# Attention with squared ReLU and a gated unit in one kernel: loads of v issued tile by tile, tile 24 and two loads of z moved, and another order of work at the end

## The chip, the cores and the metric

The kernel runs on one core of one Trainium2 chip. The metric is device time of one execution in microseconds (us); lower is better. Inputs and outputs are float32.

## The reference

For 8 batches of 3200 rows, v and u have 256 columns and z has 64. The scores are z times z transposed, so they are symmetric; their squared ReLU is multiplied with v, and the result, multiplied by u, goes through a short causal convolution, a sigmoid gate and two 256x256 projections.

```python
scores = (1.0 / S) * np.matmul(z, z.transpose(0, 2, 1))
attn = np.maximum(scores, 0.0) ** 2
x = u * np.matmul(attn, v)
xp = zeros of 4 rows, then x
gate = sigmoid(sum over k of conv_w[k] * xp[:, k : k + S, :])     # 5 taps
out = (gate * (x @ w_val)) @ w_out
```

## The kernel before, in words

The 3200 rows of a batch are 25 tiles of 128 rows. Queries are handled in six main chunks of 4 tiles (512 columns), numbered 0 to 5, and a last tile, number 24, which is a chunk of its own (number 6, `ONE`). For each main chunk the keys are walked in pairs of tiles; such a pair is a step, so a chunk has 13 steps. The last main chunk of a batch (5) has 16, since the three steps of chunk 6, marked S, are mixed into it.

Every float32 operand is held as a high part (rounded to the fast float32 form, `fp32r`) and a low part (the remainder), and each product is three products of parts. ScalarE (ACT) makes the high parts by a cast, VectorE (DVE) the low parts by a subtraction. For the weights of attention these are the tiles `ah` and `al`, for v `v_hl`, for z `zhl`, for x `xh` and `xl`, for the gated value `gvh` and `gvl`.

Since the scores are symmetric, the kernel computes a block once, transposes it (`turned`), stores it to DRAM (`mir`) and fetches it back later as `m` for the chunk on the other side. `m_fetch` issues that fetch six steps before the block's use; ACT casts it and DVE makes its remainder three steps before the use.

The order of all work is written out by hand. `at_step(s, fn, ...)` puts small work behind step s, and every engine runs its instructions in program order. Nearly all DMAs are issued by one queue, SyncE's (SP). A load, cast or remainder is placed by these tables, as steps relative to the start of a chunk:

- `Z_FROM[b][c]`: the step, relative to the first step of batch b, at which chunk c of z is loaded (`z_load`, four issues through `blocks_load`, L161). Its transpose by DVE (`z_turn`, L215), its cast (`z_high`) and its remainder (`z_low`, L231) follow 3, 4 and 5 steps later, for batch 1 4, 5 and 6. All z loads of batches 1 to 7 use one buffer, `z_raw`.
- `V_LOAD`: the step, relative to the start of the last main chunk of the batch before, at which tiles of v are loaded (`v_load_at`, down to `v_rows`, L356), and whether into a small buffer `v_raw` or into one of 8 tiles that shares the buffers of `turned` (`v_raws`).
- `V_HIGH`: the same for the cast of pair i of v by ACT (`v_high`, L410); the remainder by DVE (`v_low`, L415) follows one step later. Entry 12 is tile 24. For batch 1, steps above 13 count one more.

`v_rows` loads m neighbouring tiles of v with rows interleaved in blocks of 32: one issue for each of the four blocks of partitions.

The two chunks before are finished beside the attention of the current one: product with u, convolution taps (`conv`, L811), sigmoid, value product, gate, projection. The single tiles are finished in groups of batches (`one_...`). After the last steps of the last batch, the end is written out step by step: the last four steps' products are made for the left and the right 256 columns apart, so that the taps of the left half run beside the products of the right half; then value, gate, projection of the last chunk, the projection of the chunk before (`project_whole`, L972) and that of the last single tile.

Of the kernel before, what the change touches and what calls it, by code (L numbers as in the profile page):

```python
# [11 lines left out]
ALU = mybir.AluOpType  # L12
P = 128
BLK = 32
# [3 lines left out]
def attn_glu_kernel(  # L18
# [29 lines left out]
    nc = tc.nc  # L48
    B, S, D = u.shape
# [11 lines left out]
    sizes = [4] * n_chunks + [1]  # L61
    firsts = [4 * c for c in range(n_chunks + 1)]
# [13 lines left out]
    def f32(ap):  # L76
        return ap.bitcast(F32)
# [273 lines left out]

    def v_rows(dst, b, g, t, m):

        for a in range(P // BLK):
            k = firsts[g] * P + (a * sizes[g] + t) * BLK
            nc.sync.dma_start(  # L356
                dst[a * BLK : (a + 1) * BLK], v[b, k : k + m * BLK, :].rearrange("(t r) d -> r t d", r=BLK)
            )
# [78 lines left out]
    turned = {}  # L437
# [298 lines left out]
    u_raw, ut = {}, {}  # L736
# [21 lines left out]
    def gated(b, c, h, cols=ALL, with_=None):  # L758
        opened = (b, c) in xs
        if not opened:  # L760
            xs[b, c] = sb.tile([P, DH, X_ROW], F32, name="x", bufs=1)
        x = xs[b, c]
        nc.vector.tensor_tensor(  # L763
            x[:, h, HALO + cols.start : HALO + cols.stop], accs[b, c][h][:, cols] if with_ is None else with_, ut[b, c][:, h, cols], op=ALU.mult
        )
        if not opened:
            x_halo(b, c)
# [20 lines left out]
    def x_high(b, c, hs=slice(0, DH), cols=ALL):  # L788
        if (b, c) not in xhl:
            xhl[b, c] = (  # L790
                sb.tile([P, DH, CW], F32R, name="xh", bufs=1),
                sb.tile([P, DH, CW], F32R, name="xl", bufs=1),
            )
        nc.scalar.copy(xhl[b, c][0][:, hs, cols], xs[b, c][:, hs, HALO + cols.start : HALO + cols.stop])
# [7 lines left out]
    def conv(b, c, h, k, first=None, cols=ALL):  # L802
        x, cw = xs[b, c], weights["conv"]
        if (b, c) not in gates:
            gates[b, c] = sb.tile([P, DH, CW], F32, name="gate", bufs=1)
        g = gates[b, c][:, h, cols]
        tap = x[:, h, k + cols.start : k + cols.stop]
        if k == 0:
            (first or nc.scalar.mul)(g, tap, cw[:, h, 0:1])  # L809
        else:  # L810
            nc.vector.scalar_tensor_tensor(g, tap, cw[:, h, k : k + 1], g, op0=ALU.mult, op1=ALU.add)  # L811
# [44 lines left out]
    def value_part(b, c, h, cols, banks):  # L856
        wh, wl = weights["val"]
        xh, xl = (x[:, h, cols] for x in xhl[b, c])
        for terms in (((wl, xh), (wh, xh)), ((wh, xl),)):
            for e in range(DH):  # L860
                for wp, xp in terms:
                    ends = h == DH - 1 and xp is xl
                    nc.tensor.matmul(
                        banks[e][:, : CW // 2], wp[:, h, e * P : (e + 1) * P], xp, start=h == 0 and wp is wl, stop=ends
                    )
# [9 lines left out]
        nc.scalar.copy(gvs[b, c][0][:, e, cols], gv)  # L875
        return gv

    def gate_part_low(b, c, e, cols, gv):
        gvh, gvl = (x[:, e, cols] for x in gvs[b, c])
        nc.vector.tensor_tensor(gvl, gv, f32(gvh), op=ALU.subtract)  # L880

    def project_tiles(b, c, tiles_, banks):
        wh, wl = weights["out"]
# [79 lines left out]
    def project_whole(b, c, banks):  # L963
        pos[b, c] = banks
        lists = [project_list(b, c, x, True, True) for x in range(DH)]

        n = sizes[c]
        early = [3 if turned_out(b, c) else 3 * (n // 2 + (x == 0) * (n % 2)) for x in range(DH)]
        for part in range(2):
            for mms, e in zip(lists, early):  # L970
                for out_, st, mv, first, last in mms[e:] if part else mms[:e]:
                    nc.tensor.matmul(out_, st, mv, start=first, stop=last)  # L972
# [335 lines left out]
    def fill_at(s, fn, *args):  # L1308
# [23 lines left out]
    }  # L1332
    FIRST_LAST = {6: 9, 7: 10, 8: 11, 9: 12, 10: 12}

    Z_FROM = {b: (-53, -48, -41, -33, -22, -10, -15) if b > 1 else (-17, -40, -35, -31, -24, -9, -5) for b in range(1, B)}

    U_LOAD = ((6, -1, -8, -11, -8, -8), (1, -2, -2, -9, -8, -8))
    U_PREP = ((11, 2, 1, 2, 4, 6), (10, 10, 3, 4, 4, 6))
# [2 lines left out]
        (-9, (20, 21, 22, 23), None),  # L1341
        (-6, (14, 15, 16, 17), None),
        (2, (0, 1, 2, 3), (0, 0)),
        (3, (24,), (1, 6)),
        (4, (4, 5, 6, 7), (0, 4)),
        (6, (8, 9, 10, 11), (1, 0)),
        (8, (12, 13), (1, 4)),
        (16, (18, 19), None),
    )
    V_HIGH = (7, 8, 9, 10, 11, 12, 13, 16, 17, 18, 14, 15, 6)  # L1350

    CONVERSIONS = (
        (2, 2, convert_conv(), 10),
# [117 lines left out]
    with tc.manual_schedule():  # L1471
# [13 lines left out]
        for s in range(min(todo), END + 1):  # L1485
# [86 lines left out]
            if s == END:  # L1572

                b, c = LAST
                g = len(GROUPS) - 1
                assert (b, c) not in xhl and (b, c) not in gates
                one_products(g, (0, 1, 2))
                left_, right = slice(0, CW // 2), slice(CW // 2, CW)
                pending, sums = [], []
                for cols in (left_, right):  # L1580
                    for h in range(DH):
                        attend_part(steps[s:], h, cols, None if cols is left_ else apart[h][:, : CW // 2])
                        if cols is left_ and h == 0:
                            one_value_whole(g)
                            apart = two_banks(False)
                        if cols is left_:
                            gated(b, c, h, cols)
                        else:
                            nc.vector.tensor_tensor(sums[h], apart[h][:, : CW // 2], sums[h], op=ALU.add)
                            gated(b, c, h, cols, sums[h])  # L1590
                        x_high(b, c, one[h], cols)
                        if cols is left_ and h == 0:
                            one_value_copy(g)
                            one_products(g, (3, 4))
                        for fn, *args in pending:
                            fn(*args)
                        if cols is right:
                            one_halo_last(b, h)
                        conv(b, c, h, 0, nc.scalar.mul if (cols is left_) == (h == 1) else nc.vector.tensor_scalar_mul, cols)
                        if (cols, h) == (right, 1):  # L1600
                            break
                        if cols is left_:
                            sums.append(sb.tile([P, CW // 2], F32, name="sum", tag=("z_raw", "u_raw")[h], bufs=1))
                            nc.scalar.copy(sums[h], accs[b, c][h][:, right])
                        for k in range(1, KW):
                            conv(b, c, h, k, cols=cols)
                        sigmoid(b, c, one[h], cols)
                        pending = [(x_low, b, c, one[h], cols)]
                value_l, value_r = (s_bank_pair(x) for x in (next_s[0], 1 - next_s[0]))
                for h in range(DH):  # L1610
                    value_part(b, c, h, left_, value_l)
                value_part(b, c, 0, right, value_r)
                conv(b, c, 1, 1, cols=right)
                x_low(b, c, one[1], right)
                value_part(b, c, 1, right, value_r)
                project_whole(b, c - 1, two_banks(False))
                lefts = [gate_part(b, c, e, left_, value_l, "a") for e in range(DH)]
                one_conv_first(g)
                for k in range(2, KW):
                    conv(b, c, 1, k, cols=right)  # L1620
                sigmoid(b, c, one[1], right)
                one_sigmoid(g)
                for e in range(DH):
                    gate_part_low(b, c, e, left_, lefts[e])
                rights = [gate_part(b, c, e, right, value_r, ("gv", "zz")[e]) for e in range(DH)]
                one_gated_last(g)
                one_gated_high(g)
                for e in range(DH):
                    gate_part_low(b, c, e, right, rights[e])
                one_gated_low(g)  # L1630
                for x in range(DH):
                    out_copy(b, c - 1, x)
                out_store(b, c - 1)
                lefts = s_bank_pair(next_s[0])
                project_tiles(b, c, (0, 1), lefts)
                tiles_out(b, c, (0, 1), lefts, ("z_raw", "u_raw"), (nc.scalar.copy,) * 2, (nc.sync,) * 2)
                rights = two_banks(True, "acc")
                project_tiles(b, c, (2, 3), rights)
                one_project_whole(g, s_bank_pair(1 - next_s[0]))
                tiles_out(b, c, (2, 3), rights, ("ut", "turned"), (nc.vector.tensor_copy, nc.scalar.copy), (nc.scalar, nc.scalar))  # L1640
                one_out(g)


# [31 lines left out]
```

## Time and profile before

| what | value |
|---|---|
| median of 3 runs | 2258.09 us (2257.62 to 2263.52) |
| the profiled execution | 2262.12 us, span 2260.3 us |
| granted TensorE clock | 1.000 |
| DVE, ACT, POOL busy | 82%, 76%, 3% of the span |
| SP's waits of at most | 15.0 us (L542, for a `turned` tile) |
| loads of v of 64 KB and 32 KB | 100 + 28 and 28 + 4 issues |

In rows of the timeline the first number is the start in us from the start of the span, the second the duration; then come engine, line, operation, tile written and tiles read, and their shapes; `x4` means four instructions merged. In brackets stands how long the engine was idle before and what released it. SPq is SP's queue, PEld a weight load of TensorE. In rows of waits stand the engine and line that waited, whom for, and us in total, how often, and the longest. In rows of DMA issues the median time from issue to landing stands last.

### The profile page before, as it was taken

How to read it: one execution, taken by the hardware profiler on the slowest of the kernel's cores; microseconds unless marked ns; L12 is line 12 of the kernel's file. 1: busy time of each engine (PE TensorE's matmuls, PEld its weight loads, DVE VectorE, ACT ScalarE, POOL GpSimd, SP SyncE). 2: the span in 40 equal slices, each digit the busy share in tenths (PEclk: the TensorE clock that was granted, in tenths of full speed). 3: DMA queues.
4: the chain of work that ended last, by engine and by line, in shares of the span. 5: the costliest groups of instructions: out<-in, count | busy, mean ns of one | idle time of the engine just before them, and what ended most of it. 6: DMA issues, size and time to landing. Idle time of an engine off the chain costs nothing.

```text
span 2260.3 us, 50037 instructions
## 1 busy us (share of the span) xinstructions
PE 2247.4 (99%) x20311; PEld 1911.3 (85%) x20311; DVE 1852.5 (82%) x2296; ACT 1707.4 (76%) x2145; POOL 76.6 (3%) x119
## 2 busy tenths in 40 slices
PE   9999999999999999999999999999999999999998
PEld 7888888889888988888988888888898888888888
DVE  8877788887889778887888968888788887888776
ACT  8987688766887668876688766987669776697764
POOL 0000000000000000000000000000000000000000
PEclk9999999999999999999999999999999999999999
DMA  5557857887677876788667776777858778677663
GB/s 123 117 135 159 205 136 164 184 197 205 150 163 181 189 200 150 169 185 193 182 164 168 189 185 177 166 177 183 206 144 184 173 181 206 148 184 172 170 179 98
DMA packets 700600, 386.61 MB, mean 171 GB/s; under 512 B 411856, under 2 KB 635088, under 8 KB 700368
## 3 DMA queue, kind: packets, MB, share of 16 engines
q1 hardware_dynamic: 699024, 383.01, 71.4%
q8 instruction: 159, 2.61, 0.5%
q14 instruction: 73, 0.60, 0.1%
q10 hardware_dynamic: 1344, 0.39, 0.1%
HBM read 211.82 MB, written 171.44 MB: 170 GB/s over the span
## 4 chain that ended last, share of the span: by engine, by line
PE 92%; SPq 2%; DVE 2%; DMA 2%; ACT 1%; issue 1%; ACTq 0%; DVEq 0%
PE acc L428 67%; PE s L428 12%; PE misc L428 11%; DMA m<-mir 1%; SPq L356 1%; DVE al L649 1%; PE acc L733 1%; SPq L161 1%; SPq L1044 0%; DVE gate L811 0%; DMA z_raw<-in_z_dram 0%; DMA v_raws<-in_v_dram 0%; ACT ah L643 0%; SPq L555 0%; DVE x L763 0%
## 5 line engine op out<-in xcount | busy, mean ns | idle before, releaser
L428 PE MATMUL acc<-ah,v_hl 64*128 64x512 f32 x9472 | 1606.9, 388 | 1.2 <-DVE x L763 0.6
L428 PEld LDWEIGHTS acc<-ah,v_hl 64*128 64x128 f32 x9472 | 942.9, 184 | 165.0 <-issue 1.5
L428 PE MATMUL acc<-al,v_hl 64*128 64x512 f32 x4736 | 965.0, 387 | 2.1 <-DVE al L649 2.0
L428 PEld LDWEIGHTS acc<-al,v_hl 64*128 64x128 f32 x4736 | 480.9, 184 | 83.6 <-DVE al L649 4.8
L649 DVE TENSOR_TENSOR al<-a,ah 128x1024 fp32r<-128x1024 f32 (+1 forms) x346 | 398.3, 1151 | 184.5 <-ACT ah L643 182.7
L640 ACT ACTIVATE a<-s 128x1024 f32<-128x1024 f32 (+1 forms) x346 | 333.0, 963 | 137.5 <-PE s L428 122.8
L643 ACT CAST ah<-m 128x1024 fp32r<-128x1024 f32 x254 | 264.9, 1047 | 154.4 <-PE acc L428 83.0
L641 ACT ACTIVATE a<-a 128x1024 f32<-128x1024 f32 (+1 forms) x346 | 347.7, 1005 | 11.0
L649 DVE TENSOR_TENSOR al<-m,ah 128x1024 fp32r<-128x1024 f32 x254 | 307.8, 1212 | 53.7 <-ACT ah L643 53.6
L643 ACT CAST ah<-a 128x1024 fp32r<-128x1024 f32 (+1 forms) x323 | 319.9, 990 | 10.2
L520 DVE STREAM_TRANSPOSE turned<-a 128x1024 f32<-128x1024 f32 (+1 forms) x278 | 318.5, 1146 | 0.1
L811 DVE SCALAR_TENSOR_TENSOR gate<-x,cw,gate 128x512 f32<-128x512 f32 (+1 forms) x392 | 284.7, 726 | 4.9 <-ACT gate L809 1.1
L428 PE MATMUL s<-zq,zhl 64*128 64x512 f32 (+1 forms) x1596 | 222.5, 378 | 1.6 <-DVE gv L1065 1.6
L428 PEld LDWEIGHTS s<-zq,zhl 64*128 64x128 f32 x1596 | 153.0, 184 | 30.0 <-DVE gv L1065 2.0
L763 DVE TENSOR_TENSOR x<-acc,ut 128x512 f32<-128x512 f32 (+1 forms) x96 | 61.4, 681 | 83.4 <-PE acc L428 70.5
L815 ACT ACTIVATE gate<-gate 128x512 f32<-128x512 f32 (+1 forms) x98 | 60.9, 622 | 71.1 <-DVE gate L811 70.8
L913 ACT CAST gvh<-gv 128x512 fp32r<-128x512 f32 x94 | 58.2, 620 | 38.0 <-DVE gv L909 37.9
L428 PE MATMUL misc<-xh,w_val_hi 64*128 64x512 f32 x376 | 77.2, 386 | 0.0
L428 PE MATMUL misc<-xh,w_val_lo 64*128 64x512 f32 x376 | 77.2, 386 | 0.0
L428 PE MATMUL misc<-xl,w_val_hi 64*128 64x512 f32 x376 | 77.2, 386 | 0.0
L428 PE MATMUL s<-v_hl,ah 64*128 64x512 f32 x400 | 76.3, 394 | 0.0
L909 DVE TENSOR_TENSOR gv<-misc,gate 128x512 f32<-128x512 f32 x94 | 64.5, 686 | 12.7 <-PE misc L428 8.3
(197 smaller groups left out, 2021.7 us busy)
## 6 DMA issues: line engine op xcount, KB each, us to landing
mir<-turned SPq DMA_DIRECT2D x460, 256.0 KB, 4.1
m<-mir SPq DMA_DIRECT2D x230, 512.0 KB, 4.9
u_raw<-in_u_dram SPq DMA_DIRECT2D x384, 64.0 KB, 3.5
mir<-turned SPq DMA_DIRECT2D x376, 64.0 KB, 2.5
m<-mir SPq DMA_DIRECT2D x94, 256.0 KB, 4.6
out_dram<-ob SPq DMA_DIRECT2D x152, 128.0 KB, 3.6
v_raws<-in_v_dram SPq DMA_DIRECT2D x100, 128.0 KB, 3.7
z_raw<-in_z_dram SPq DMA_DIRECT2D x182, 64.0 KB, 3.2
```

The lines of the kernel that those rows point to most:

```text
L161: queues[i % len(queues)].dma_start(dst[i * BLK : (i + 1) * BLK], src[:, d0 : d0 + BLK].rearrange("(j c) r -> c j r", c=BLK),)
L428: ins = nc.tensor.matmul(out_, st[r], mv[r], start=first, stop=last)
L520: nc.vector.transpose(into[:, t : t + m], a[:, j * w : (j + m) * w].rearrange("p (t m x) -> p t m x", t=m, x=BLK))
L640: nc.scalar.activation(a[:, : n * w].rearrange("p (j x) -> p j x", j=2), s[:, :, :each], AF.Relu, scale=scale)
L641: nc.scalar.activation(a, a, AF.Square)
L643: nc.scalar.copy(hi, a)
L649: nc.vector.tensor_tensor(lo, a, f32(hi), op=ALU.subtract)
L763: nc.vector.tensor_tensor(x[:, h, HALO + cols.start : HALO + cols.stop], accs[b, c][h][:, cols] if with_ is None else with_, ut[b, c][:, h ...
L811: nc.vector.scalar_tensor_tensor(g, tap, cw[:, h, k : k + 1], g, op0=ALU.mult, op1=ALU.add)
L815: nc.scalar.activation(g, g, AF.Sigmoid)
L909: nc.vector.tensor_tensor(gv[:, :w], pvs[b, c][e][:, :w], gates[b, c][:, e, :w], op=ALU.mult)
L913: nc.scalar.copy(gvs[b, c][0][:, e, :w], gv_[b, c, e][:, :w])
```

## The change

It does four things.

1. `v_rows` has a new path for runs shorter than 4 tiles: one issue for each tile, with all 128 partitions, in place of one for each block of 32 partitions.
2. Tile 24 of v is loaded with tiles 18 and 19 at step 16, the first step of the next batch, into `v_raw`, and no longer at step 3 of the last chunk; its cast goes from step 6 to step 19.
3. For batch 1, the load of z for chunk 0 goes from step -17 to step -15, and that for chunk 6 from step -5 to step -20. Their transposes, casts and remainders follow.
4. At the end: the tap 0 that ACT makes goes ahead of the cast of xh; the projection of the chunk before (`project_whole`) goes between the value products of the left and the right half; the remainders of the left gated value go from DVE to GpSimd (POOL); the third tile's projection is stored before the single tile's projection, on SP, and the fourth's comes last, copied by DVE.

```diff
     def v_rows(dst, b, g, t, m):
+        if m < P // BLK:
+            for x in range(m):
+                k = firsts[g] * P
+                rows_ = v[b, k : k + sizes[g] * P, :].rearrange("(a t r) d -> t a r d", t=sizes[g], r=BLK)[t + x]
+                nc.sync.dma_start(dst[:, x], rows_)
+            return
         for a in range(P // BLK):
...
-    def gate_part_low(b, c, e, cols, gv):
+    def gate_part_low(b, c, e, cols, gv, engine=nc.vector):
         gvh, gvl = (x[:, e, cols] for x in gvs[b, c])
-        nc.vector.tensor_tensor(gvl, gv, f32(gvh), op=ALU.subtract)
+        engine.tensor_tensor(gvl, gv, f32(gvh), op=ALU.subtract)
...
-    Z_FROM = {... else (-17, -40, -35, -31, -24, -9, -5) ...}
+    Z_FROM = {... else (-15, -40, -35, -31, -24, -9, -20) ...}
...
-        (3, (24,), (1, 6)),
...
-        (16, (18, 19), None),
+        (16, (18, 19, 24), None),
     )
-    V_HIGH = (7, 8, 9, 10, 11, 12, 13, 16, 17, 18, 14, 15, 6)
+    V_HIGH = (7, 8, 9, 10, 11, 12, 13, 16, 17, 18, 14, 15, 19)
...
+                        on_scalar = (cols is left_) == (h == 1)
+                        if on_scalar:
+                            conv(b, c, h, 0, nc.scalar.mul, cols)
                         x_high(b, c, one[h], cols)
...
-                        conv(b, c, h, 0, nc.scalar.mul if (cols is left_) == (h == 1) else nc.vector.tensor_scalar_mul, cols)
+                        if not on_scalar:
+                            conv(b, c, h, 0, nc.vector.tensor_scalar_mul, cols)
...
                     value_part(b, c, h, left_, value_l)
+                project_whole(b, c - 1, two_banks(False))
                 value_part(b, c, 0, right, value_r)
                 conv(b, c, 1, 1, cols=right)
                 x_low(b, c, one[1], right)
                 value_part(b, c, 1, right, value_r)
-                project_whole(b, c - 1, two_banks(False))
...
-                    gate_part_low(b, c, e, left_, lefts[e])
+                    gate_part_low(b, c, e, left_, lefts[e], nc.gpsimd)
...
-                project_tiles(b, c, (2, 3), rights)
+                project_tiles(b, c, (2,), rights[:1])
+                tiles_out(b, c, (2,), rights[:1], ("ut",), (nc.vector.tensor_copy,), (nc.sync,))
                 one_project_whole(g, s_bank_pair(1 - next_s[0]))
-                tiles_out(b, c, (2, 3), rights, ("ut", "turned"), (nc.vector.tensor_copy, nc.scalar.copy), (nc.scalar, nc.scalar))
+                project_tiles(b, c, (3,), rights[1:])
                 one_out(g)
+                tiles_out(b, c, (3,), rights[1:], ("turned",), (nc.vector.tensor_copy,), (nc.scalar,))
```

More of the change, by code (lines that the diff above doesn't have):

```diff
@@ L1333, in attn_glu_kernel @@
     FIRST_LAST = {6: 9, 7: 10, 8: 11, 9: 12, 10: 12}
-    Z_FROM = {b: (-53, -48, -41, -33, -22, -10, -15) if b > 1 else (-17, -40, -35, -31, -24, -9, -5) for b in range(1, B)}
+    Z_FROM = {b: (-53, -48, -41, -33, -22, -10, -15) if b > 1 else (-15, -40, -35, -31, -24, -9, -20) for b in range(1, B)}
     U_LOAD = ((6, -1, -8, -11, -8, -8), (1, -2, -2, -9, -8, -8))
```

## The prediction

> **What bounds the kernel now.** I read the page first, then the waits of PE, then the timeline of PE at the few places where it waits, and from each place back along ACT, DVE and SP. The page says that TensorE is the bound almost everywhere:
>
> ```profile
> span 2260.3 us, 50037 instructions
> PE 2247.4 (99%) x20311; PEld 1911.3 (85%) x20311; DVE 1852.5 (82%) x2296; ACT 1707.4 (76%) x2145; POOL 76.6 (3%) x119
> ```
>
> No product is added or removed by the change, so only PE's idle time, and the work behind the last product, can be won. The waits of PE (who was waited for: us in total, times, longest) set the ceiling:
>
> ```profile
> PE acc L428 <- DVE al L649: 2.0, 3, 0.8
> PE s L428 <- DVE gv L1065: 1.6, 1, 1.6
> PE misc L435 <- DVE zeros L1473: 1.5, 1, 1.5
> PE s L863 <- DVE xl L798: 0.6, 1, 0.6
> PE acc L428 <- DVE x L763: 0.6, 3, 0.2
> ...
> ```
>
> That is 6.3 us in the rows shown, 1.5 of it the first memset, which stays. 0.3% of 2258 is 6.8 us, about what a measurement of this kernel can tell from no change; even a perfect edit hardly reaches it. PE's timeline shows where the idle time lies (start, duration, form, idle before and its releaser):
>
> ```profile
> 270.05 0.39 PE L428 MATMUL s<-v_hl,al 64*128 64x256 f32 x2 [0.29 <-DVE al L649]
> 272.78 0.50 PE L428 MATMUL acc<-al,v_hl 64*128 64x512 f32 x2 [0.82 <-DVE al L649]
> 278.54 0.38 PE L428 MATMUL s<-v_hl,al 64*128 64x256 f32 x2 [0.18 <-DVE al L649]
> 289.58 0.73 PE L428 MATMUL s<-zq,zhl 64*128 64x512 f32 x4 [1.58 <-DVE gv L1065]
> 1396.22 0.50 PE L428 MATMUL acc<-al,v_hl 64*128 64x512 f32 x2 [0.38 <-DVE al L649]
> 1673.29 0.50 PE L428 MATMUL acc<-al,v_hl 64*128 64x512 f32 x2 [0.76 <-DVE al L649]
> ```
>
> Four of the six, 2.87 us, lie in the last chunk of batch 0, where batch 1 is fetched; the other two, 1.14 us, at the same place before batches 5 and 6. All six come late in the last chunk, and the ACT and SP rows of that place say why:
>
> ```profile
> 246.09 1.05 ACT L643 CAST ah<-m 128x1024 fp32r<-128x1024 f32 x1 [4.09 <-DMA m<-mir]
> 267.31 0.41 ACT L410 CAST v_hl<-v_raws 128x256 fp32r<-128x256 f32 x1 [7.08 <-DMA v_raws<-in_v_dram]
> 233.87 4.85 SPq L356 DMA_DIRECT2D v_raw<-in_v_dram  x8
> 246.49 3.33 SPq L161 DMA_DIRECT2D z_raw<-in_z_dram  x4
> 262.12 2.90 SPq L356 DMA_DIRECT2D v_raws<-in_v_dram  x4
> 278.77 3.36 SPq L356 DMA_DIRECT2D v_raws<-in_v_dram  x4
> 282.86 2.08 SPq L161 DMA_DIRECT2D z_raw<-in_z_dram  x4
> ```
>
> The 0.41 us cast of tile 24 (128x256) held ACT's queue for 7.08 us, because its four loads were issued only at 262.12 on a late SP queue. Behind it in ACT's order stood the casts whose al PE missed at 270.05 and 272.78.
>
> **The change part by part.**
>
> *Loads of v by tile.* One issue per tile of 128 rows replaces four per run of one or two tiles: in batches 1 to 7, 20 issues become 9 (runs 14-15, 16-17, 12-13, 18-19, and 24); in batch 0, 20 become 9 as well. Before tile 14, 8 issues took 4.85 us; 4 at the same 0.61 take 2.4, and SP is 2.4 us earlier for the mirror fetches behind. 12-13 saves half of 3.36, 1.7 us.
>
> What such a load costs until it lands, no row shows: a source of four blocks of 32 rows in one issue does not occur. The nearest are the 32-row and 64-row loads:
>
> ```profile
> v_raws<-in_v_dram SPq DMA_DIRECT2D x28, 32.0 KB, 3.3
> q1 hardware_dynamic: 699024, 383.01, 71.4%
> ```
>
> Lower end: it lands like these, 3.3 us after issue, and the saved issues are a gain. Upper end: its four blocks are served four wide. From the queue row (packets, MB, share of 16 engines), 0.714 x 16 x 2260.3 us for 383 MB is 67 ns of one DMA engine for each KB; a 131 KB tile is 8.8 engine-us, 0.55 us over 16 engines and 2.2 us over four. I take the lower end for my sum, with something kept for the start, since most landing times are waits and not transfer; the upper end is rival one. The Trainium skill, "DMA: Bandwidth & Descriptors", section "Why a DMA increments its semaphore by 16 and not by 1", has a rule that speaks for the upper end: a transfer uses the largest number of engines up to 16 that divides the outermost dimension of both sides. By it a source of four blocks would run on four engines; nothing in this trace shows such a transfer, so it stays a rival.
>
> *At the start* the loads feed DVE:
>
> ```profile
> 3.05 2.03 SPq L356 DMA_DIRECT2D v_raw<-in_v_dram  x4
> 6.65 0.43 DVE L410 CAST v_hl<-v_raw 128x512 fp32r<-128x512 f32 x1
> 8.92 0.69 DVE L231 TENSOR_TENSOR zhl<-misc,zhl 128x512 fp32r<-128x512 f32 x1 [1.11 <-ACT zhl L226]
> 18.52 0.42 DVE L410 CAST v_hl<-v_raw 128x512 fp32r<-128x512 f32 x1
> ```
>
> Tiles 0 and 1 are cast at 6.65, and DVE then idles 1.11 us, which covers that much lateness. Two issues instead of four end 1.0 us earlier. Gain to -0.3; loss at four engines: eight tiles, 17.6 us in a row from 3.05, end at 20.7 at the earliest, and at 24 with the 3.3 us to land; the last pair is cast at 18.52, so 2 to 5 late. I take +0.3.
>
> *Tile 24.* Its load leaves SP at step 3 of the last chunk (2.90 us there) and joins 18 and 19 at step 16; cast and remainder move from steps 6 and 7 to 19 and 20. ACT's 7.08 us wait goes; late next are the mirror casts behind it, which wait for their own fetches, and those are issued earlier by the 2.9 us. The price is 0.41 us on ACT and 0.42 on DVE in the next first chunk, and one more tile behind 18-19. There the cover is:
>
> ```profile
> 578.92 0.79 SPq L356 DMA_DIRECT2D v_raw<-in_v_dram  x2
> 585.17 0.63 ACT L410 CAST v_hl<-v_raw 128x512 fp32r<-128x512 f32 x1
> ```
>
> 6.25 us from the first issue to the cast, against 3.3 to land and 0.6 for each issue: hidden, and tile 24 has one step more. If that cover went, the 0.8 us of casts would cost up to 0.4 a batch.
>
> *Two z loads of batch 1.* Chunk 0's load (four issues, 3.33 us) goes from before the last chunk to step 1 of it, chunk 6's (2.08 us) from step 11 of the last chunk to step 9 of the chunk before. SP's order then: chunk 6's four issues stand before the first mirror fetch of the last chunk, whose cast at 246.09 began as its DMA landed, so a delay there passes on. It is 2.08 late against 2.4 early from tiles 14 to 17: nothing. Everything behind 246.49 moves 3.3 us forward up to step 1, where the load now stands. Its transpose on DVE moves two steps:
>
> ```profile
> 254.46 0.71 DVE L215 STREAM_TRANSPOSE zz<-z_raw 128x512 f32<-128x512 f32 x1
> 261.04 0.69 DVE L231 TENSOR_TENSOR zhl<-zz,zhl 128x512 fp32r<-128x512 f32 x1
> ```
>
> The transpose will stand about where the remainder stood, 261.0. It took at most 8.0 us from first issue (246.49) to transpose; from an issue at 250 to 254 it is ready at 258 to 262: DVE waits 0 to 1 us, and the remainders of the mirrors wait behind it. The z work of chunk 6, operands a quarter of chunk 0's, moves into the last chunk.
>
> Joint: between -2.9 (all four idle times go) and +1.0 (none goes and the transpose waits). The 1.58 at 289.58 hangs on the last mirror fetches, behind 278.77 and 282.86; SP is lighter there by 2.9 + 1.7 us ahead of them, so I take -2.9 in the profiled run. Before batches 5 and 6 the same ACT wait goes: -1.1, or 0.
>
> *The end.*
>
> ```profile
> 2240.51 2.05 DVE L811 SCALAR_TENSOR_TENSOR gate<-x,cw,gate 128x256 f32<-128x256 f32 x4 [0.55 <-ACT gate L809]
> 2244.23 2.05 DVE L811 SCALAR_TENSOR_TENSOR gate<-x,cw,gate 128x256 f32<-128x256 f32 x4 [0.55 <-ACT gate L809]
> 2247.46 0.51 PE L863 MATMUL s<-xl,w_val_hi 128*128 128x256 f32 x2 [0.63 <-DVE xl L798]
> 2237.44 0.72 POOL L1161 TENSOR_TENSOR one_sum<-one_sum,one_terms 128x248 f32<-128x248 f32 x1 [1.91 <-ACT one_terms L1159]
> 2237.55 0.89 DVE L811 SCALAR_TENSOR_TENSOR gate<-x,cw,gate 128x256 f32<-128x256 f32 x1
> 2256.69 0.66 SPq L1267 DMA_DIRECT2D out_dram<-one_f  x1
> ```
>
> Twice DVE waits 0.55 us for ACT's gate product, because ACT casts xh first. With the order turned DVE starts up to 0.55 earlier each time, I take 0.4, 0.8 in all; xh has PE's remaining sums ahead of it. Putting the 24 products of the chunk before between the halves of the value hides the 0.63 of 2247.46. Moving two remainders to POOL takes 0.75 off DVE and puts two operations of about 0.72 on POOL; but beside a POOL operation a tap took 0.89, where four take 2.05 (0.51 each), so up to 0.4 for each of two comes back. The third tile's output now precedes the single tile's, which overlaps copies. The last store, 2256.69, moves forward by the 0.63 and part of the 0.8. Bounds -1.3 and +0.3; I take -0.8. The Trainium skill, "SBUF — State Buffer", section "SBUF: two separate sides", says that such a VectorE operation with two inputs in SBUF and a GpSimd operation exclude each other, the second one waiting in full. By it 0.7 would come back for each and the end would gain 0.3; the trace agrees with a wait, and its 0.4 decides.
>
> **Sum.** The profiled execution took 2262.12 us (span 2260.3). -2.9 - 1.1 - 0.8 + 0.3 = -4.5: 2257.6 on that footing. The median of the runs is 2258.09, 4.0 lower, as much as the six idle times together, and two of these stand at only two of seven like places; so I credit the median with half of them: 2258.1 - 2.0 - 0.8 + 0.3 = **2255.6**.
>
> **The rivals.**
>
> One, slower: the one-issue tiles are served by four engines. Place: the start, and each last chunk's first mirror fetch, which follows tiles 14 to 17.
>
> ```profile
> 1064.40 3.78 SPq L356 DMA_DIRECT2D v_raw<-in_v_dram  x8
> 1073.28 1.05 ACT L643 CAST ah<-m 128x1024 fp32r<-128x1024 f32 x1 [1.57 <-DMA m<-mir]
> 1077.15 1.22 DVE L649 TENSOR_TENSOR al<-m,ah 128x1024 fp32r<-128x1024 f32 x1
> 1079.60 0.61 PE L428 MATMUL acc<-al,v_hl 64*128 64x512 f32 x2
> ```
>
> Four tiles hold four engines for 8.8 us instead of 2.2; less 1.9 of saved issuing, the fetch lands up to 4.7 us later. ACT's cast starts as it lands and ends at 1074.33, DVE uses it at 1077.15: 2.8 are covered. It decides from there; up to 1.9 us pass on to the remainder, which ends at 1078.37 and is used by PE at 1079.60, 1.2 later: 0 to 0.7 a batch, I say 0.5 in six. With +2.5 at the start and my other terms: 2258.1 + 3 + 2.5 - 2.8 = 2260.8.
>
> Two, nothing happens in the middle: runs without a profiler have few of these waits, and the gain is the end's: 2258.1 - 0.8 + 0.3 = 2257.6. For it speaks that only batch 1 waits for more than a microsecond; against it, ACT's 7.08 us is a queue order and not chance.
>
> Three, all of it is won in the median too: 2258.1 - 4.0 - 1.3 - 0.3 = 2252.5.
>
> **How the numbers follow.** Forecast 0.50, four engines 0.25, nothing in the middle 0.13, all won 0.12. All four lie within 0.3% (2251.3 to 2264.9). Slower than that takes the upper ends of rival one (5 at the start, 0.7 in six batches and no gain elsewhere: 2267.3): 0.07. Faster takes more than PE's removable idle time: 0.05. Same: 0.88. The range reaches from a little below "all won" to the middle of rival one: 2251.8 to 2261.
>
> **What would show it.** Right: no ACT wait for v_raws near 260 to 267, PE without idle at 269 to 290, DVE's waits for the gate product gone from the end, SP issuing 72 small loads of v and not 160. Wrong: landing times of the 128 KB v loads far above the 64 KB ones, new PE idle within the first 25 us or near the first mirror fetches, a DVE transpose of z waiting for its DMA near 261, or taps near 0.9 us beside POOL until PE waits in the last products.

## The result, and the profile after

| kernel | median | ratio to before (95% interval) |
|---|---|---|
| before | 2258.09 us (2257.62 to 2263.52) | |
| after | 2282.9 us (2280.9 to 2285.64) | 1.0103 (1.009 to 1.0117) |

The change makes the kernel 24.8 us slower; the prediction was 2255.6 us, 2261 at the most. In what follows, each ratio, and each "over" or "under before" of a median, is against runs of the kernel before made beside the kernel named (medians 2258.09 to 2260.13 us); one run of both_old_loads, 2787.72 us at a granted clock of 0.752, is left out of its ratio. The profiled execution of the changed kernel took 2285.64 us, its span 2283.8. As in the page of before, TensorE works all the time but for waits; it has 7 us more busy time and lost the rest in idle time:

```profile
span 2283.8 us, 49919 instructions
PE 2254.6 (99%) x20311; PEld 1914.3 (84%) x20311; DVE 1854.4 (81%) x2295; ACT 1705.6 (75%) x2144; POOL 76.2 (3%) x121
```

PE's waits of after. Lines of after are 6 above those of before from L356 on to the gate's functions, so L428 is L434 here, L649 is L655, L1065 is L1071:

```profile
PE s L434 <- DVE gv L1071: 8.3, 7, 3.0
PE acc L434 <- DVE al L655: 5.7, 8, 0.8
PE s L434 <- DVE al L655: 3.1, 4, 1.4
PE misc L441 <- DVE zeros L1478: 1.4, 1, 1.4
PE acc L434 <- DVE ah L585: 1.2, 1, 1.2
PE misc L202 <- DMA z_rows<-in_z_dram: 1.0, 1, 1.0
PE acc L434 <- ACT ah L649: 0.7, 2, 0.5
PE acc L895 <- ACT gvh L881: 0.6, 1, 0.6
```

The wait for `gv`, once 1.6 us in the whole kernel, now comes seven times, once before each of batches 1 to 7. Behind it stands ACT's wait for the mirror fetches (`m<-mir`); first the row of before, then that of after:

```profile
ACT ah L643 <- DMA m<-mir: 53.8, 41, 4.4
```

```profile
ACT ah L649 <- DMA m<-mir: 126.6, 54, 6.6
```

ACT's wait for `v_raws`, 29.8 us in before, is gone, as it should be; 72.8 us of waiting for mirror fetches came in. To see where PE loses time, take from each trace the start of the first product of v with the remainder `al` in every main chunk. A joint is the stretch from that of chunk 5 to that of the next batch's chunk 0, so it holds the last chunk, and "start" is that of batch 0's chunk 1 (us, worked out from the PE rows of each trace; before and after are the two profiled executions):

| | start | joint 1 | 2 | 3 | 4 | 5 | 6 | 7 | from batch 7's chunk 5 to the end |
|---|---|---|---|---|---|---|---|---|---|
| before | 56.7 | 57.95 | 53.00 | 52.71 | 52.99 | 53.39 | 54.30 | 52.71 | 66.49 |
| after | 59.7 | 63.03 | 55.59 | 54.64 | 57.30 | 53.75 | 57.10 | 55.33 | 66.83 |

3.0 us are lost at the start, 19.7 over the seven joints, 0.3 at the end; the chunks between the joints agree within 0.5 us in all. So the time is lost where the new loads of v are; tile 24 and the two z loads were moved at the same places, and the experiments below separate them.

What the DMA engines do there shows in 40 slices of a window (first row: busy share of the 16 engines in tenths; second: GB/s). Of after, 8 to 14 us, while it loads the first tiles of v:

```profile
DMA  2233333222222222235995322225994222223996
GB/s 77 77 84 67 72 73 87 77 92 94 96 96 89 96 96 89 89 99 143 212 196 126 105 89 89 96 89 133 230 210 123 89 89 89 96 96 113 207 228 135
```

Between bursts of other transfers the 16 engines stand at two to three tenths and some 94 GB/s, as they would with four of sixteen at work. Packet by packet the trace agrees: between 9.0 and 10.4 us four to seven packets are under way at any moment, four most often. A tile of 131 KB at that rate takes 1.4 us. The profile gives no landing times for this kernel (its rows of DMA issues end with the size), where that of before had them.

### The profile page after: what moved, and what is told of

Same layout as the page of the kernel before. It is cut to its first block, busy times and chain, and to the rows that moved or that the text cites. A ratio compares the mean times of both kernels' runs of the same rounds, so it can differ in the third digit from the quotient of the medians.

```text
span 2283.8 us, 49919 instructions
## 1 busy us (share of the span) xinstructions
PE 2254.6 (99%) x20311; PEld 1914.3 (84%) x20311; DVE 1854.4 (81%) x2295; ACT 1705.6 (75%) x2144; POOL 76.2 (3%) x121
## 4 chain that ended last, share of the span: by engine, by line
PE 80%; DMA 7%; DVE 5%; SPq 3%; ACT 2%; issue 1%; DVEq 0%; POOL 0%; POOLq 0%; ACTq 0%
PE acc L434 59%; PE misc L434 10%; PE s L434 10%; DMA m<-mir 4%; DVE al L655 2%; DMA v_raws<-in_v_dram 2%; SPq L161 1%; ACT ah L649 1%; DVE gate L817 1%; DMA z_raw<-in_z_dram 1%; DMA v_raw<-in_v_dram 1%; PE acc L739 1%; SPq L1050 0%; SPq L358 0%; DVE turned L526 0%
## 5 line engine op out<-in xcount | busy, mean ns | idle before, releaser
L434 PE MATMUL acc<-ah,v_hl 64*128 64x512 f32 x9472 | 1610.8, 388 | 3.2 <-DVE ah L585 1.2
L434 PEld LDWEIGHTS acc<-ah,v_hl 64*128 64x128 f32 x9472 | 945.7, 184 | 167.1 <-ACT ah L649 2.9
L434 PE MATMUL acc<-al,v_hl 64*128 64x512 f32 x4736 | 969.5, 388 | 5.9 <-DVE al L655 5.7
L434 PEld LDWEIGHTS acc<-al,v_hl 64*128 64x128 f32 x4736 | 482.4, 184 | 88.1 <-DVE al L655 9.9
L655 DVE TENSOR_TENSOR al<-a,ah 128x1024 fp32r<-128x1024 f32 (+1 forms) x346 | 396.8, 1147 | 191.3 <-ACT ah L649 190.2
L649 ACT CAST ah<-m 128x1024 fp32r<-128x1024 f32 x254 | 265.0, 1047 | 218.1 <-DMA m<-mir 126.6
L655 DVE TENSOR_TENSOR al<-m,ah 128x1024 fp32r<-128x1024 f32 x254 | 307.8, 1212 | 69.8 <-ACT ah L649 67.4
L649 ACT CAST ah<-a 128x1024 fp32r<-128x1024 f32 (+1 forms) x323 | 319.9, 990 | 10.3
L434 PE MATMUL s<-zq,zhl 64*128 64x512 f32 (+1 forms) x1596 | 223.6, 380 | 8.3 <-DVE gv L1071 8.3
L434 PEld LDWEIGHTS s<-zq,zhl 64*128 64x128 f32 x1596 | 151.8, 185 | 39.7 <-DVE gv L1071 11.3
L434 PE MATMUL misc<-xh,w_val_hi 64*128 64x512 f32 x376 | 77.6, 386 | 0.0
L434 PE MATMUL misc<-xl,w_val_hi 64*128 64x512 f32 x376 | 77.6, 386 | 0.0
L434 PE MATMUL misc<-xh,w_val_lo 64*128 64x512 f32 x376 | 77.6, 386 | 0.0
L434 PE MATMUL s<-v_hl,ah 64*128 64x512 f32 x400 | 76.2, 393 | 0.0
```

The lines of the kernel that those rows point to most:

```text
L434: ins = nc.tensor.matmul(out_, st[r], mv[r], start=first, stop=last)
L649: nc.scalar.copy(hi, a)
L655: nc.vector.tensor_tensor(lo, a, f32(hi), op=ALU.subtract)
```

## The experiments

**Undo one part, do one part.** The first kernel is the changed one without the new path of `v_rows`; the second is the kernel before with that path alone (the first hunk of the diff).

> The changed kernel with the small loads of v as they were: four issues of 32 rows a tile (part one undone), the other three parts kept. Theory (a load of a whole tile from four blocks runs on four of the 16 DMA engines, and the late mirror fetches of each last chunk stand behind it): the loss of 24.8 us goes, 2253 to 2258, and ACT's wait for the mirror fetches falls from 126.6 back to about 54 us. Rival (tile 24's move or the z loads of batch 1 make the loss): 2270 to 2283.

> The kernel before with the one-issue loads of v alone. Theory of the four engines: 2280 to 2288, the start 3 us later and 20 us over the seven joints. Rival (the other parts make the loss): 2256 to 2260.

Measured: with the old loads 2263.72 us, ratio 1.0017 (1.0007 to 1.0026); with the new loads alone 2279.11, 1.0089 (1.0073 to 1.0104). The loads of v make 20.1 of the 24.8 us, and their kernel loses 3.2 at the start and 10.8 in the joints of its profiled execution, the fastest of its four runs. The kernel with the old loads came out 5.7 us above its expected range: the other three parts do not win anything, and together they cost 1.6 to 5.9 us by the interval of that ratio. In its profiled execution that loss is not to be seen (joints 376.6 us in all, 377.1 in before).

**One issue from one block, from eight, from two.** The first is the changed kernel, the other two are the kernel before, each with another source or split of the new path. With one block and with eight, the tiles get other rows of v than the reference's, so these two kernels are for timing alone.

```diff
-   rows_ = ....rearrange("(a t r) d -> t a r d", t=sizes[g], r=BLK)[t + x]       # four blocks of 32 rows
+   k = (firsts[g] + t + x) * P;  rows_ = v[b, k : k + P, :]                      # one_block
+   rows_ = ....rearrange("(a t r) d -> t a r d", t=sizes[g], r=BLK // 2)[t + x]  # eight_blocks
+   for y in range(2): nc.sync.dma_start(dst[64 * y : 64 * y + 64, x], rows_[2 * y : 2 * y + 2])   # two_blocks
```

> The changed kernel, but each small tile of v is read as one contiguous block of 128 rows instead of four blocks of 32; as many issues and as many bytes. The rows of v that these tiles hold are then others than the reference's. Theory of the four engines (the four blocks make four engines): the transfer spreads over all 16, 2253 to 2258, with landings near 3 us. Rival (one issue of 64 KB a tile is slow whatever its source, or SP's order is what costs): 2278 to 2285.

> The kernel before with each small tile of v as one issue of eight blocks of 16 rows (the rows that the tiles hold are then others than the reference's). Theory (as many engines as blocks): eight engines, half the backlog of four; the start costs 0 to 1 us and the joints 0 to 1 us each, 2258 to 2266. Rival (the cost of a scattered source comes from the number of its pieces, so eight pieces are worse than four): 2279 or more.

> The kernel before with each small tile of v loaded in two issues of two blocks of 32 rows each; half as many issues as before for these tiles. Theory (as many engines as blocks): each issue runs on two engines, so the backlog is at least as long as with four: 2290 to 2350. Rival (what costs is the size of an issue or their number): between the two kernels, 2258 to 2272.

| blocks in the source of one issue | kernel | median | ratio (95%) |
|---|---|---|---|
| 1 | one_block | 2261.34 us | 1.0009 (0.9999 to 1.0018) |
| 8 | eight_blocks | 2262.5 us | 1.0011 (1.0002 to 1.002) |
| 4 | rows_only | 2279.11 us | 1.0089 (1.0073 to 1.0104) |
| 2 | two_blocks | 2360.09 us | 1.0445 (1.043 to 1.0461) |

One block and eight cannot be told apart, and the kernel of one block also has the other three parts of the change. From two blocks to eight, more pieces take less time: it is not the scatter that costs but the width. Two blocks keep the engines at one tenth, 46 GB/s, with two to four packets under way (10 to 18 us):

```profile
DMA  1111111111111111111111111111111111111111
GB/s 46 46 41 51 40 44 38 44 38 40 45 37 44 41 51 41 46 46 46 46 46 46 41 51 41 51 41 51 41 51 41 51 41 46 46 46 46 41 51 46
```

A single block fills them (4 to 10 us), and its one-issue loads, as large and as many as those of after, land in 2.9 and 3.7 us:

```profile
DMA  9999987997777965699999795698999986699879
```

```profile
v_raws<-in_v_dram SPq DMA_DIRECT2D x114, 128.0 KB, 3.7
v_raw<-in_v_dram SPq DMA_DIRECT2D x86, 128.0 KB, 2.9
```

46 GB/s for two blocks, 94 for four: 23 GB/s for each block. The expectation for two blocks, at most 2350, was 10 us too low, that for one block, at most 2258, 3.3 too low; eight blocks came out as expected. The rule of the Trainium skill, "DMA: Bandwidth & Descriptors", section "Why a DMA increments its semaphore by 16 and not by 1", that the outermost sizes of both sides set the number of engines, agrees with the rates of two and four blocks and with the times of two, four and eight.

**Where the loss is.** The kernel before with the new path under one condition each: batch 0 only, tiles 14 to 17 only, tiles 12 and 13 only.

> The kernel before with the one-issue loads of v in batch 0 alone (tiles 0 to 11 by pairs, now 12 issues of a tile on four engines). By the prediction's rival (2.5 us at the start) and the profile after (3.0 us): 2261 to 2263. Rival (the start's 3 us are given back at the joint of batch 1, where the next late operand waits anyway): 2259 to 2260.

> The kernel before with the one-issue loads of v for tiles 14 to 17 of batches 1 to 7 alone. By the prediction (2.8 us of backlog are covered, 0 to 0.7 a batch): 2258 to 2264. Theory now (the backlog of 512 KB on four engines isn't worked off in the busy last chunk and is still there at its late mirror fetches): 2266 to 2274. Rival (the loss comes from tiles 12 and 13, which are loaded two steps ahead of those fetches): 2259 to 2262.

> The kernel before with the one-issue loads of v for tiles 12 and 13 of batches 1 to 7 alone. Theory of a backlog that tiles 14 to 17 carry through the chunk: these two alone (256 KB, some 3 us on four engines) cost less, 2260 to 2265. Rival (they are the cause, being nearest to the late mirror fetches): 2270 to 2278.

Measured: the start 2264.55 us (1.0022, 1.0012 to 1.0032), 4.9 over before; tiles 14 to 17 2268.27 (1.0043, 1.0027 to 1.0058), 8.6 over; tiles 12 and 13 2266.5 (1.0034, 1.0021 to 1.0048), 6.9 over. Together 20.4, as rows_only's 20.1. (In batch 0 the new path takes tiles 0 to 7 and 24, nine issues, not the twelve of the expectation.) The shares are rough: by the intervals the start costs 2.7 to 7.2 us, tiles 14 to 17 6.1 to 13.1, tiles 12 and 13 4.7 to 10.8, and the profiled execution of tiles 14 to 17, the fastest of its five runs, shows only 1.8 us more in the joints. Nor are they even: of the 6.3 us that tiles 12 and 13 add to the joints of their profiled execution, 4.6 lie in joint 1 and 2.0 in joint 2, and 1.3 of the 4.6 is a longer wait of PE for `al` at 271.5, ahead of their issue, so not theirs. Tiles 12 and 13 cost more than I expected of them, so neither the backlog of 14 to 17 nor the rival has the joints for itself.

**Place in the queue.** The trace of the kernel with tiles 12 and 13 shows the path. In before, the last mirror fetch of the joint is issued at 282.23, and its cast begins as it lands, 4.4 us later:

```profile
282.23 0.52 SPq L555 DMA_DIRECT2D m<-mir  x1
286.61 1.06 ACT L643 CAST ah<-m 128x1024 fp32r<-128x1024 f32 x1 [0.82 <-DMA m<-mir]
```

With tiles 12 and 13 on four engines right ahead of it, it lands 8.1 us after its issue. DVE's remainder waits for that cast, `gv` stands behind the remainder, and PE idles 3.32 us for `gv`:

```profile
280.31 1.31 SPq L358 DMA_DIRECT2D v_raws<-in_v_dram  x2
281.72 0.57 SPq L561 DMA_DIRECT2D m<-mir  x1
289.77 1.04 ACT L649 CAST ah<-m 128x1024 fp32r<-128x1024 f32 x1 [2.76 <-DMA m<-mir]
290.85 1.23 DVE L655 TENSOR_TENSOR al<-m,ah 128x1024 fp32r<-128x1024 f32 x1 [2.17 <-ACT ah L649]
291.99 0.68 DVE L1071 TENSOR_TENSOR gv<-s,gv 128x512 f32<-128x512 f32 x1
292.73 0.96 PE L434 MATMUL s<-zq,zhl 64*128 64x512 f32 x6 [3.32 <-DVE gv L1071]
```

So two kernels issue the same tiles just behind the fetch that stood behind them, and one gives the tiles a queue of their own:

```diff
-        (8, (12, 13), (1, 4)),
+        (10, (12, 13), (1, 4)),          # behind_12_13
-        (-6, (14, 15, 16, 17), None),
+        (-5, (14, 15, 16, 17), None),    # behind_14_17
-                nc.sync.dma_start(dst[:, x], rows_)
+                (nc.scalar if b else nc.sync).dma_start(dst[:, x], rows_)   # act_queue
```

> The kernel before with tiles 12 and 13 of batches 1 to 7 as one-issue loads (which alone cost 6.9 us), and these two issued two steps later in the last chunk, behind the mirror fetch that followed them. Theory of the order (the fetch right behind the tiles waits for them): the 6.9 us fall to 0 to 2.5, 2258 to 2262. Rival (the time they take of four engines counts wherever they stand): 2264 to 2268. Tiles that now come too late themselves would show as ACT waiting for v_raws, and cost more.

> The kernel before with tiles 14 to 17 of batches 1 to 7 as one-issue loads (which alone cost 8.6 us), issued one step later, so that the mirror fetch that stood right behind them goes first. Theory of the order: that fetch lands in time and the loss falls to 2 to 5 us, 2261 to 2265, the fetches further behind still being late. Rival (a backlog on four engines that lasts through the chunk): 2266 to 2271.

> The kernel before with the one-issue loads of v, those of batches 1 to 7 issued by ACT instead of SP. Theory one (the fetches stand behind the tiles in SP's own rings, and SP is held by the eight landings that it counts): with a queue of their own the tiles share the four engines by turns with the fetches, and the 17 us of the joints fall to under 8, 2261 to 2270. Theory two (the four engines serve whatever came first, of any queue): 2275 to 2282. Should ACT itself be held at these issues, the joints cost more, over 2282.

Behind the fetch, tiles 12 and 13 cost nothing: 2259.38 us, 0.9997 (0.9988 to 1.0006), where they had cost 6.9 us. The fetch, now issued ahead of them, is cast 3.8 us earlier, though ACT still waits 1.46 for it, and PE's wait for `gv` at this joint falls from 3.3 to 0.4:

```profile
277.82 3.02 SPq L561 DMA_DIRECT2D m<-mir  x2
280.89 1.32 SPq L358 DMA_DIRECT2D v_raws<-in_v_dram  x2
285.98 1.05 ACT L649 CAST ah<-m 128x1024 fp32r<-128x1024 f32 x1 [1.46 <-DMA m<-mir]
```

Tiles 14 to 17 fall from 8.6 to 3.3 us: 2263.43, 1.0018 (1.0009 to 1.0028), which just touches the interval at the old place (1.0027 to 1.0058). For tiles 12 and 13 the order theory holds; for 14 to 17 the runs agree with it. That the 3.3 us left come from later fetches behind those four tiles is not shown.

The queue of ACT does not decide between the first two theories: 2354.07 us, 1.0419 (1.0397 to 1.0441), the third case of its expectation. ACT itself is held at the issues, and the chunks between the joints, which no other kernel here with loads from four blocks touches by more than 0.5 us, grow by 59.6 us over batches 1 to 7. The program counts all its DMAs on eight semaphores, and in the trace an issue waits for the landing of the DMA that had its semaphore before. On SP that holds up a queue; on ACT it holds up its casts. Here ACT ends a cast at 517.79, can issue only at 524.55, and goes on working at 527.12; the row of waits counts four such places (how much of the 59.6 us comes of this is not worked out):

```profile
517.17 0.62 ACT L919 CAST gvh<-gv 128x512 fp32r<-128x512 f32 x1 [1.29 <-DVE gv L915]
524.55 2.52 ACTq L358 DMA_DIRECT2D v_raw<-in_v_dram  x4
527.12 0.60 ACT L646 ACTIVATE a<-s 128x512 f32<-128x512 f32 x1 [9.33 <-DMA v_raw<-in_v_dram]
```

```profile
ACT a L646 <- DMA v_raw<-in_v_dram: 36.2, 4, 9.3
```

**The other three parts, one by one**, each in the kernel before (hunks of the diff: `Z_FROM`; `V_LOAD` and `V_HIGH`; the end).

> The kernel before with the two z loads of batch 1 moved and nothing else. By the prediction's step (the joint of batch 1 gains up to 2.9 us, with tile 24's wait gone as well): 2256 to 2258. Theory now, from the run with the old loads of v (its joint of batch 1 came out at +0.03 us): the wait there passes to the next late operand, no change, 2258 to 2260. Rival: the load of chunk 6's z moved 15 steps earlier takes DMA time from the mirror fetches and costs 1 to 4 us.

> The kernel before with tile 24 alone loaded and cast with the next first chunk. By the prediction: ACT's wait of 7.1 us per batch goes, no cost elsewhere, 2256 to 2258. Rival: ACT reaches its other work sooner but PE's waits at the joints have another cause, no change, 2258 to 2260. Second rival: the load of tile 24 at step 16 lies in front of other loads, or its cast in front of others' on ACT, and costs 0.4 us a batch, 2261 to 2264.

> The kernel before with the edits of the last chunk alone. By the prediction's term: 0.8 us less, 2257 to 2258.3. By the profile of the run with the old loads of v (from batch 7 chunk 5 on, 0.32 us more): 2258.5 to 2259.5. Rival: 2 to 5 us more, since the runs with the old loads of v are 4.7 us above before while their profiled execution is not.

| kernel | median | ratio (95%) | joint 1 | from batch 7's chunk 5 to the end |
|---|---|---|---|---|
| z_only | 2260.99 us | 1.0006 (0.9997 to 1.0015) | 57.23 us | 66.55 us |
| tile24_only | 2261.44 us | 1.0005 (0.9996 to 1.0014) | 58.92 us | 66.53 us |
| end_only | 2260.51 us | 1.0003 (0.9994 to 1.0011) | 55.64 us | 66.80 us |

None gains, and none can be told from no change (z_only and end_only came out 1 us above what I expected of them by then). By the medians they stand 1.1, 1.6 and 0.6 us over before, 3.3 together. Tile 24's move does what it says: ACT's 29.8 us of waiting for `v_raws` are gone, but its wait for mirror fetches grows from 53.8 to 71.3:

```profile
ACT ah L643 <- DMA m<-mir: 71.3, 43, 3.9
```

That growth is not one execution's chance alone: five kernels with tile 24 and the loads of v in the joints as they were have 46.2 to 57.7 us there, the kernel with the old loads and tile 24 moved has 67.5. With the loads from one block it is 49.6.

Joint 1 of end_only is the surprise. This kernel is the kernel before up to batch 7, yet its joint 1 took 2.3 us less, and that of another such kernel (end_gvl_dve, below) 0.5 less. The joint varies from execution to execution.

**The end.** The edits of the end, with the two subtractions `gvl` of the left half back on DVE:

```diff
-                    gate_part_low(b, c, e, left_, lefts[e], nc.gpsimd)
+                    gate_part_low(b, c, e, left_, lefts[e])
```

> The kernel before with the edits of the end, but the two subtractions gvl of the left half on VectorE as they were, not on GpSimd. Theory (GpSimd's two subtractions slow VectorE beside them: its five small products took 1.05 us instead of 0.47, three taps 1.85 instead of 1.52, two subtractions 1.10 instead of 0.76 while GpSimd ran): the stretch from the last chunk on comes out 0.2 to 0.8 us under that of the kernel before instead of 0.3 over. Rival (the order of the products makes the 0.3): +0.3 or more. In the whole time 2257 to 2260, which a run can hardly tell from no change; the profile's stretch decides.

The stretch to the end is 65.95 us: 0.54 under before's, where it is 0.31 over with GpSimd. In the whole time 2258.96 us, 0.9996 (0.9987 to 1.0005). The rows show why. DVE beside GpSimd, in end_only:

```profile
2245.12 1.05 DVE L1168 TENSOR_TENSOR one_f<-one_f,cw 128x8 f32<-128x8 f32 x5
2245.39 1.45 POOL L880 TENSOR_TENSOR gvl<-gv,gvh 128x256 fp32r<-128x256 f32 x2 [1.93 <-ACT gvh L875]
2246.31 1.85 DVE L811 SCALAR_TENSOR_TENSOR gate<-x,cw,gate 128x256 f32<-128x256 f32 x3
2249.26 0.39 PE L889 MATMUL acc<-w_out_lo,gvh 128*128 128x256 f32 x1 [0.59 <-ACT gvh L875]
2250.06 0.39 PE L889 MATMUL acc<-w_out_hi,gvl 128*128 128x256 f32 x1 [0.30 <-DVE gvl L880]
```

and without it, in end_gvl_dve:

```profile
2247.95 0.47 DVE L1168 TENSOR_TENSOR one_f<-one_f,cw 128x8 f32<-128x8 f32 x5
2248.57 1.52 DVE L811 SCALAR_TENSOR_TENSOR gate<-x,cw,gate 128x256 f32<-128x256 f32 x3
2250.47 0.39 PE L889 MATMUL s<-w_out_hi,gvl 128*128 128x256 f32 x1 [0.16 <-DVE gvl L880]
```

DVE's own work took 0.58 and 0.33 us longer while GpSimd ran for 1.45, 0.91 in all; that delays the sum of taps that the sigmoid waits for, and PE waits 0.9 in its last products. The stretch repeats well: 66.80 to 66.83 us in the four kernels with GpSimd there, 65.86 to 65.99 in the three without it, 66.36 to 66.55 in the twelve with the old end.

**What is left, put together**: the end's order with `gvl` on DVE, and tiles 12 and 13 at the later step, once as one issue each and once with the old four.

> The kernel before with the end's edits (gvl on VectorE), and tiles 12 and 13 of batches 1 to 7 as one issue each, two steps later, behind the mirror fetch. By the two alone (0.9996 and 0.9997): 2257 to 2260, 0 to 2 us under the kernel before, at or under what can be told from no change; the stretch from the last chunk on 0.5 us shorter.

> As the other, but tiles 12 and 13 in four issues of 32 rows each as before, at the same later step. If the place counts: as the other, 2257 to 2260. If the number of issues counts (eight instead of two on SP): 1 to 3 us above the other, with SP's later issues of mirror fetches held up.

Measured: 2258.49 us, 0.9994 (0.9985 to 1.0003), and 2259.34 us, 0.9995 (0.9986 to 1.0004). The two cannot be told apart, so at this place no effect of the number of issues shows. Neither version is faster than the kernel before by what can be measured; only the stretch at the end, 65.86 and 65.99 us against 66.49, is surely shorter.

## Why the prediction was wrong

**The step that failed** is "Loads of v by tile", in "I take the lower end for my sum". A source of four blocks does not land like the 32-row and 64-row loads; its width is that of rival one. The reason given, that most landing times are waits and not transfer, fitted the loads that the trace had rows of (0.55 us of 3.3 by the prediction's own figures); for a load on four engines it leaves out 1.4 us of transfer a tile, and with it the lateness of everything behind in the queue. In place of the +0.3 that the sum had for these loads, the runs show 20.1 us.

**Rival one** had the mechanism and a chance of a quarter, but its price was too low: 2260.8. Its time per tile was even too high (2.2 us estimated, 1.4 measured at 94 GB/s). What it missed was who waits. It followed only the first mirror fetch behind tiles 14 to 17, and let 2.8 us of cover absorb it: 0.5 us in six batches, 3 in all; these tiles cost 8.6 (1.2 a batch on average). Tiles 12 and 13, two issues right ahead of the last mirror fetch, it counted as saved issue time alone; they cost 6.9 (1.0 a batch on average). The start's 2.5 were 3.0 in the profiled execution and 4.9 in the medians. In place of 5.5 us stand 20; the measured time lies beyond even the rival's upper end, 2267.3.

**At the start** +0.3 was taken, 2 to 5 for four engines; the upper end's reasoning was right in size.

**Tile 24**: ACT's wait of 7.08 us went as said, and its gain did not come. The step named what is late next, the mirror casts, and trusted that their fetches would be earlier; instead 17.5 of ACT's 29.8 us came back as waits for exactly these in tile24_only, and the rest gained no time that can be measured.

**Two z loads**: -2.9 was priced from four idle times of one execution. Two executions of the same code up to batch 7 have joint 1 at 55.64 and 57.47 us against its 57.95: it varies by 2.3 us with no edit, nearly the size of the term. With the loads moved, z_only has 57.23, inside that spread, so no gain shows. The prediction had the sign of it in hand (4.0 us between its own time and the median, "as much as the six idle times together") and still credited half. Rival two, nothing happens in the middle, was right in its outcome for these two parts; its reason, that runs without a profiler have few of these waits, is not tested by any run.

**The end**: the waits for the gate product fell from 0.55 to about 0.27 each, not by 0.4, and the 0.63 of `xl` went, as said; with the remainders left on DVE the stretch came out 0.54 shorter. Against that, DVE lost 0.91 beside GpSimd, about the 0.8 that the step allowed, and it lost them ahead of the sigmoid, on the path of the last products, where the step had set them off as if elsewhere. The stretch came out at the bound, +0.3. The Trainium skill, "SBUF — State Buffer", section "SBUF: two separate sides", lets the second of two such operations wait in full; the runs show a wait, 0.91 us beside GpSimd's 1.45. By the prediction's terms that rule (0.7 in place of 0.4 for each of two) gives about -0.2, where the prediction says a gain of 0.3: nearer to the measured +0.3 than its own -0.8, but not its sign.

Of the signs named: PE idle within the first 25 us and near the mirror fetches, and slow DVE work beside POOL, came as written under "wrong"; the gone wait for `v_raws` as written under "right". Landing times, another of the signs, the profile of after does not give.

Open is where the 1.6 to 5.9 us of the three other parts together go: each alone is within what can be told, 0.6 to 1.6 us over before, 3.3 in sum, and the profiled executions are too uneven in the joints to place them. The kernel with one block, which has the three parts too, is at 1.0009 (0.9999 to 1.0018), so part of that cost may be the old loads beside them.

## What to carry to other kernels

Fewer and larger loads cost time when each spreads over fewer DMA engines, and here they gained nothing measurable even when spread over all: look at the shape of the source and not at the bytes, and at the busy share in a window where only that load runs. Price a slower load by everything queued behind it until the queue is empty, above all the transfer issued right behind, not by the first waiter alone. Before an idle time in one profiled execution is counted as a gain, ask whether it stands at every like place; one that stands at two of seven may be that execution's and not the program's.

## What the runs showed of the hardware that was not expected

The time grows much faster than the width falls: 2.6, 20 and 101 us over before in the medians for eight, four and two blocks. In the profiled executions the joints lose nothing with eight (375.2 us in all against 377.1), 10.8 us with four and 72.5 with two.

An idle PE can pay twice. After 3.04 us without work, in the first joint of after, the granted clock falls and the next products run slower:

```profile
296.30 1.65 PE L434 MATMUL s<-zq,zhl 64*128 64x512 f32 x6 [3.04 <-DVE gv L1071]
```

The windows of after (start, end and length in us; busy time and instructions of PE, PEld, DVE, ACT, POOL; then the granted clock, the DMA share and GB/s):

```profile
0.00:12.00 12.00, 8.37 (x35) 5.88 (x37) 4.70 (x9) 4.21 (x6) 1.31 (x10) 1.00 0.52 114
12.00:16.00 4.00, 4.00 (x20) 2.92 (x22) 3.93 (x8) 3.38 (x8) 0.00 (x0) 0.57 0.51 116
16.00:20.00 4.00, 4.00 (x37) 3.37 (x37) 3.65 (x6) 3.93 (x4) 0.00 (x0) 1.00 0.64 153
296.00:300.00 4.00, 3.70 (x20) 3.00 (x22) 3.93 (x7) 3.35 (x4) 0.00 (x0) 0.60 0.00 0
300.00:304.00 4.00, 4.00 (x44) 3.41 (x44) 2.13 (x5) 2.52 (x4) 0.00 (x0) 1.00 0.33 68
```

In the same stretch of before, behind an idle time of 1.58 us, the clock stays at 1.00. At the start of after PE was without work for 3.6 of the first 12 us, against 2.0 in before, and behind the first memset its longest waits before the clock fell are 0.97 and 1.21 us. So the length of one wait does not decide: in rows_only PE waits 2.81 us at 295.22, and the clock from there to 299 stays at 1.00. Four microseconds at 0.57 are up to 1.7 us lost on top, more than half of the 3.0 at the start, and at 0.60 1.6 of the first joint's 5.1; together 3.3 of the 7.2 us that PE is busy longer.
